# A common tag for the DRAM scratch tensors of cast queries and keys, in a banded-attention and SwiGLU kernel

## The chip, the cores and the metric

The kernel runs on one core of a Trainium2 chip. The metric is the device time of one execution in microseconds (us). Before the change it is 375.43 us, the median of five runs (374.43 to 377.87 us).

## The reference

There are two stages. The first is attention over 8 batches of 8 heads, with 576 positions of 64 numbers each. A query sees the keys within 32 positions of itself and the 8 global positions, and a global query sees every key. The second is a gated feed-forward block over the 4608 rows that result.

```
mask = (abs(pos[:, None] - pos[None, :]) <= 32) | is_global[:, None] | is_global[None, :]
scores = where(mask, q @ k.T / sqrt(64), -1e9)
attn = softmax(scores);  o = attn @ v                    # per batch and head
x = o.transpose(0, 2, 1, 3).reshape(8 * 576, 512)
out = (silu(x @ w_gate) * (x @ w_val)) @ w_out           # 512 -> 1536 -> 512
```

## The kernel before

**Tiling.** All matmuls are in bfloat16. For each batch, `attention(b)` returns a list of steps. Step GT (L362 to L367) transposes the 8 gathered global keys and queries, held in tile `kqm`. Steps S2 and SG (L391, L373) make the scores that involve global positions. Step P2T turns the probabilities of the global queries (tile `p2t`), and step AV2 (L422) multiplies them with the values. Steps S (L452) make the scores of the band, steps AV (L496, L505) multiply with the values `va` and `vb`, and steps X turn the result into `xT`, the input of the feed-forward block. `ffn(t0, n)` takes 512 rows of `xT` at a time: 12 gate units (L638, two groups of four matmuls each) and four output units (L683), so 16 units for each of 9 chunks, 144 in all.

**Order.** The order is written by hand. A counter runs over the 144 units, and after each unit the kernel emits what the dictionary `gaps` holds for that number. Each engine keeps the order in which it was given its instructions. The tiles' pools work out which semaphores an instruction has to wait for.

**Queries and keys.** The score steps need keys and queries turned, with the 64 numbers of a head along the partitions (`kT`, `qT`). For batches 0 to 2 they are loaded into on-chip memory (L80) and turned on TensorE (L344). For batches 3 to 7 they go through DRAM. `cast_qk(b)` (L106 to L110) issues two DMAs on GpSimd's queue that read float32 keys and queries and write them in bfloat16, with positions outermost, to a scratch tensor in DRAM: `kf`, then `qf`. Later `transpose_qk(b)` (L114 to L122) issues two crossbar transposes on SyncE's queue, from `kf` to `kT` (L116) and from `qf` to `qT` (L120). `kT` has two buffers that alternate by batch, and `qT` has two by its pool.

**The scratch tensors.** The pool that they come from is made at L65 with `bufs=1` in DRAM. Before the change each request carries a name of its own (`kf3`, `qf3`, `kf4` and so on) and no tag, so there are ten tensors for five batches.

**When they are issued.** These lines place the steps around the change, by the number of the unit that they follow (`o` is 16 times b - 1):

```
cast_at, tr_at, v_at, g_at, m_at = {3: 12, 4: 25}, {3: 22}, {2: 10}, {2: 8}, {2: 15}
...
            tr_at[b] = o - 16 + 5
...
            cast_at[b] = o - 32 + 8
        v_at[b] = o - 16 + 2
        g_at[b] = o - 16 + 6
        m_at[b] = o - 16 + 13
```

So the transposes of batch b come at units 22, 37, 53, 69 and 85 for b = 3 to 7, and the casts of batches 4 to 7 come three units after the transposes of the batch ahead (25, 40, 56, 72). On GpSimd's queue a cycle is: five loads of `va` for batch b, two gathers of global rows for b (L226), the two casts for b + 1 (L109), and the two small products that make `kqm` for b (L236). GpSimd runs ahead of TensorE, as far as its waits allow. On SyncE's queue a cycle is: two copies that make `vb` (L131, L132), from batch 4 on the crossbar transpose for `p2t` (L408), the transposes of `kf` and `qf` for the next batch, the transposes for `xT` (L540, L562), and the stores of the output (L690).

Of the kernel before, what the change touches and what calls it, by code (L numbers as in the profile page):

```python
# [10 lines left out]
BF16 = mybir.dt.bfloat16  # L11
# [15 lines left out]
def kernel(  # L27
# [13 lines left out]
    B, H, S, D = q.shape  # L41
# [23 lines left out]
    dram = ctx.enter_context(tc.tile_pool(name="dram", bufs=1, space=bass.MemoryType.DRAM))  # L65
# [39 lines left out]

    def cast_qk(b):  # L106
        for name, src in (("k", k), ("q", q)):
            t = dram.tile([S, H, D], BF16, name=f"{name}f{b}")
            nc.gpsimd.dma_start(out=t, in_=src[b].rearrange("h s d -> s h d"))  # L109
            flat[name, b] = t  # L110

# [633 lines left out]
    for f, w in ((transpose_qk, tr_at), (load_v, v_at), (gather_now, g_at), (mask_now, m_at), (cast_qk, cast_at)):  # L745
        for b, n in w.items():
            at(n, f, b)
# [40 lines left out]
```

## Time and profile before

| What | Value |
|---|---|
| median of five runs | 375.43 us (374.43 to 377.87) |
| the profiled execution | 374.88 us |
| its span, first to last instruction | 373.2 us |
| TensorE busy | 346.2 us, 93% of the span |
| VectorE, ScalarE, GpSimd busy | 241.2, 150.7 and 98.2 us |
| granted TensorE clock | 1.000 |
| software DMA queue (GpSimd's) | 19.40 MB, packets take 61.3% of the 16 DMA engines' span |
| hardware DMA queue (SyncE's) | 22.74 MB, 29.7% |

The span runs from the first to the last instruction. The profiled execution took 1.68 us more than its span. A wait in the profile is idle time of an engine, put down to what ended it. A DMA's time to landing runs from its issue to the moment at which its data is complete. SPq and POOLq are the queues of SyncE and GpSimd, PE is TensorE's matmuls, PEld its weight loads, POOL is GpSimd, DVE is VectorE and ACT is ScalarE.

### The profile page before, as it was taken

The numbers are of one execution on the slowest core, as the hardware profiler recorded it, in microseconds if no ns is written. First come the engines' busy times: TensorE is split into PE (matmuls) and PEld (weight loads), VectorE is DVE, ScalarE is ACT, GpSimd is POOL, SyncE is SP. The second block draws the span as 40 slices with busy tenths as digits, with TensorE's granted clock in tenths as the row PEclk, the third lists the DMA queues.
The fourth block names the chain that finished last, engine by engine and source line by source line (L and its number), as shares of the span: only waits on it lengthen the run. The fifth ranks groups of instructions, "written<-read, shape, count | busy, mean of one in ns | idle before, by whom it ended". The sixth has DMA issues, their size and how long they took to land.

```text
span 373.2 us, 7896 instructions
## 1 busy us (share of the span) xinstructions
PE 346.2 (93%) x3224; PEld 175.2 (47%) x3276; DVE 241.2 (65%) x473; ACT 150.7 (40%) x233; POOL 98.2 (26%) x116
## 2 busy tenths in 40 slices
PE   2677999989999999998999999999999999999996
PEld 2464544554454444544554455445544554444442
DVE  5784887268951886488738872887288728724850
ACT  2643474346542652253324442454245423313321
POOL 7966267462127101370128011400000000000000
PEclk9999999999999999999999999999999999999999
DMA  8999999999975994799999998970350032011002
GB/s 117 115 198 201 184 223 140 186 209 138 94 70 85 186 146 61 139 142 149 142 144 138 148 125 141 157 128 18 113 125 2 17 111 52 0 57 58 0 25 88
DMA packets 138835, 42.64 MB, mean 114 GB/s; under 512 B 123824, under 2 KB 133040, under 8 KB 138800
## 3 DMA queue, kind: packets, MB, share of 16 engines
q0 software_dynamic: 93824, 19.40, 61.3%
q1 hardware_dynamic: 44976, 22.74, 29.7%
q8 instruction: 25, 0.41, 0.5%
q14 instruction: 10, 0.08, 0.1%
HBM read 38.28 MB, written 15.34 MB: 144 GB/s over the span
## 4 chain that ended last, share of the span: by engine, by line
PE 79%; DVE 8%; DMA 6%; ACT 3%; issue 2%; POOL 0%; DVEq 0%; POOLq 0%
PE po L683 24%; PE pg L638 21%; PE pv L638 20%; DMA p2t<-p 5%; PE ps_av L496 3%; PE ps_s L452 2%; PE ps_av L505 2%; DVE pt L465 2%; PE ps_t L344 2%; DVE h L676 1%; DMA q_bf<-in_q_dram 1%; DVE gv L672 1%; ACT pe L460 1%; PE ps_x L550 1%; DVE xa L483 1%
## 5 line engine op out<-in xcount | busy, mean ns | idle before, releaser
L638 PE MATMUL pg<-xT,wg_sb 128*128 128x512 bf16 x392 | 106.4, 380 | 3.4 <-issue 1.0
L638 PE MATMUL pv<-xT,wv_sb 128*128 128x512 bf16 x419 | 108.2, 379 | 0.2
L672 DVE SCALAR_TENSOR_TENSOR gv<-th,pg 128x512 bf16<-128x512 bf16 x108 | 74.0, 685 | 36.4 <-ACT th L670 35.5
L670 ACT ACTIVATE th<-pg 128x512 bf16<-128x512 f32 x108 | 64.4, 597 | 82.0 <-PE pg L638 78.0
L683 PE MATMUL po<-wo_sb,h 128*128 128x512 bf16 x417 | 95.5, 379 | 0.7 <-issue 0.3
L676 DVE TENSOR_TENSOR h<-gv,pv 128x512 bf16<-128x512 bf16 x108 | 74.3, 688 | 11.6 <-PE ps_av L505 0.5
L102 POOL DMA_DIRECT2D va<-in_v_dram x40 | 35.2, 913 | 117.5 <-PE ps_av L505 87.0
L638 PEld LDWEIGHTS <-wv_sb 128*128 128x128 bf16 x424 | 41.5, 98 | 50.0
L683 PEld LDWEIGHTS <-h 128*128 128x128 bf16 x432 | 40.8, 98 | 47.5
L638 PEld LDWEIGHTS <-wg_sb 128*128 128x128 bf16 x424 | 37.2, 98 | 41.9 <-issue 2.7
L688 ACT ACTIVATE osb<-po 128x512 f32<-128x512 f32 x36 | 21.5, 597 | 86.1 <-PE po L683 70.6
L460 ACT ACTIVATE pe<-ps_s 128x1024 bf16<-128x1024 f32 (+1 forms) x40 | 37.5, 939 | 17.1 <-PE ps_s L452 16.5
L465 DVE TENSOR_TENSOR pt<-pe,band 128x1024 bf16<-128x1024 bf16 (+1 forms) x40 | 25.5, 637 | 25.5 <-ACT pe L460 25.0
L477 DVE TENSOR_REDUCE den<-ps_av 128x8 f32<-128x16 f32 (+1 forms) x40 | 6.7, 168 | 36.3 <-PE ps_av L505 34.8
L483 DVE TENSOR_TENSOR xa<-ps_av,den 128x512 bf16<-128x512 f32 (+1 forms) x40 | 25.5, 638 | 1.4
L452 PE MATMUL ps_s<-qT,kT 64*128 64x64 bf16 x576 | 16.4, 196 | 3.5 <-ACT pe L460 1.5
L452 PEld LDWEIGHTS <-kT 64*128 64x128 bf16 x576 | 11.6, 98 | 16.9 <-issue 15.3
L496 PE MATMUL ps_av<-gvt,pg 128*64 128x264 bf16 x128 | 18.4, 299 | 1.0 <-DVE gvt L437 1.0
L505 PEld LDWEIGHTS <-pt 128*64 128x64 bf16 x512 | 18.0, 115 | 0.1
L505 PE MATMUL ps_av<-va,pt 128*64 128x66 bf16 x256 | 18.0, 199 | 0.0
L505 PE MATMUL ps_av<-vb,pt 128*64 128x66 bf16 x256 | 18.0, 199 | 0.0
L109 POOL DMA_DIRECT2D qf<-in_q_dram x5 | 14.1, 2826 | 0.0
(98 smaller groups left out, 219.2 us busy)
## 6 DMA issues: line engine op xcount, KB each, us to landing
out_dram<-osb SPq DMA_DIRECT2D x36, 256.0 KB, 2.0
vb<-va SPq DMA_DIRECT2D x14, 264.0 KB, 4.5
va<-in_v_dram POOLq DMA_DIRECT2D x24, 128.0 KB, 5.3
kf<-in_k_dram POOLq DMA_DIRECT2D x5, 576.0 KB, 14.4
qf<-in_q_dram POOLq DMA_DIRECT2D x5, 576.0 KB, 18.3
k_bf<-in_k_dram POOLq DMA_DIRECT2D x6, 288.0 KB, 6.6
q_bf<-in_q_dram POOLq DMA_DIRECT2D x6, 288.0 KB
va<-in_v_dram POOLq DMA_DIRECT2D x16, 96.0 KB, 4.5
```

The lines of the kernel that those rows point to most:

```text
L102: nc.gpsimd.dma_start(out=va[lo:hi, u, :, 0:D], in_=vs[t0 + lo : t0 + hi])
L452: nc.tensor.matmul(out=ps[:, par, 64 * slot : 64 * slot + 64], lhsT=kT[r : r + 64, hp, 64 * t : 64 * t + P], rhs=qTs[b][r : r + 64, hp, 64 ...
L460: nc.scalar.activation(out=pe, in_=ps[:, :, 0 : 64 * ns].rearrange("p r (s c) -> p r s c", c=64), func=AF.Exp, scale=SCALE,)
L465: nc.vector.tensor_tensor(out=pt.rearrange("p r s c -> p (r s) c"), in0=pe.rearrange("p r s c -> p (r s) c"), in1=bc(band, [[0, 2 * ns], [ ...
L483: nc.vector.tensor_tensor(out=xa.rearrange("p (g h) d -> p g h d", g=g), in0=bc(ps, pst + [[1, D]]), in1=bc(den, [[4, g], [1, 4], [0, D]]) ...
L496: nc.tensor.matmul(out=ps[64 * e : 64 * e + 64, hg], lhsT=st["pg"][:, P * tp + 64 * e : P * tp + 64 * e + 64], rhs=st["gv"].rearrange("p h ...
L505: nc.tensor.matmul(out=ps[64 * e : 64 * e + 64, hg, hl, :], lhsT=pt[:, hl % 2, 4 * (hl // 2) + 2 * (tp % 2) + e, :], rhs=(va if e == 0 els ...
L638: nc.tensor.matmul(out=ps[:, 0:n], lhsT=w[:, cc, P * fc : P * (fc + 1)], rhs=xT[:, cc, t0 : t0 + n], start=(cc == 0), stop=(cc == NCC - 1),)
L670: nc.scalar.activation(out=th[:, 0:n], in_=pg[:, 0:n], func=AF.Tanh, scale=0.5)
L672: nc.vector.scalar_tensor_tensor(out=gv[:, 0:n], in0=th[:, 0:n], scalar=1.0, in1=pg[:, 0:n], op0=ALU.add, op1=ALU.mult,)
L676: nc.vector.tensor_tensor(out=st["h"][:, fc, 0:n], in0=gv[:, 0:n], in1=pv[:, 0:n], op=ALU.mult)
L683: nc.tensor.matmul(out=po, lhsT=st["h"][:, fc, P * ts : P * (ts + 1)], rhs=wo_sb[:, fc, :], start=(fc == 0), stop=(fc == NFC - 1),)
```

## The change

The request for a scratch tensor gets a tag that is the same for all batches, `kf` for keys and `qf` for queries, and the batch's number is dropped from the name.

```
 def cast_qk(b):
     for name, src in (("k", k), ("q", q)):
-        t = dram.tile([S, H, D], BF16, name=f"{name}f{b}")
+        t = dram.tile([S, H, D], BF16, tag=f"{name}f", name=f"{name}f")
         nc.gpsimd.dma_start(out=t, in_=src[b].rearrange("h s d -> s h d"))
         flat[name, b] = t
```

Nothing else differs. In the pools of on-chip memory of this kernel, requests with one tag take turns in `bufs` buffers: `qT`, for instance, has one tag and two buffers.

More of the change, by code (lines that the diff above doesn't have):

```diff
@@ L107, in cast_qk @@
         for name, src in (("k", k), ("q", q)):
-            t = dram.tile([S, H, D], BF16, name=f"{name}f{b}")
+            t = dram.tile([S, H, D], BF16, tag=f"{name}f", name=f"{name}f")
             nc.gpsimd.dma_start(out=t, in_=src[b].rearrange("h s d -> s h d"))
```

## The prediction

> **What bounds the kernel now.** I read the shares by engine and the chain that ended last first, to see which engine an added or removed wait has to reach before it counts.
>
> ```profile
> PE 346.2 (93%) x3224; PEld 175.2 (47%) x3276; DVE 241.2 (65%) x473; ACT 150.7 (40%) x233; POOL 98.2 (26%) x116
> ...
> PE 79%; DVE 8%; DMA 6%; ACT 3%; issue 2%; POOL 0%; DVEq 0%; POOLq 0%
> PE po L683 24%; PE pg L638 21%; PE pv L638 20%; DMA p2t<-p 5%; PE ps_av L496 3%; PE ps_s L452 2%; PE ps_av L505 2%; DVE pt L465 2%; PE ps_t L344 2%; DVE h L676 1%; DMA q_bf<-in_q_dram 1%; DVE gv L672 1%; ACT pe L460 1%; PE ps_x L550 1%; DVE xa L483 1%
> ```
>
> TensorE is the bound. GpSimd holds none of the chain, and neither the casts nor the transposes of `kf` and `qf` are in it. A DMA is: `p2t<-p`, 5% of the span. Of TensorE's waits, three tell what the DMAs cost it (us in total, times, longest):
>
> ```profile
> PE ps_av L422 <- DMA p2t<-p: 1.8, 2, 1.1
> ...
> PE ps_t L344 <- DMA q_bf<-in_q_dram: 0.8, 1, 0.8
> ```
>
> No row names `kT<-kf` or `qT<-qf`. The scratch path is early enough to be unseen, and only the wait for `p2t`, 1.8 us, lies where the change could reach: the 0.8 us is at the start, before any cast. Now the two queues in time, first GpSimd's, then SyncE's, around the handover from batch 5 to batch 6 (start, length of the issue, what ended the idle time before):
>
> ```profile
> 160.43 2.33 POOL L109 DMA_DIRECT2D kf<-in_k_dram  x1
> 162.17 2.85 POOL L109 DMA_DIRECT2D qf<-in_q_dram  x1
> 163.90 1.54 POOL L236 TENSOR_TENSOR kqm<-kg,mka 128x128 bf16<-128x128 f32 x1
> 164.26 1.54 POOL L236 TENSOR_TENSOR kqm<-qg,mka 128x128 bf16<-128x128 f32 x1
> 180.16 0.82 POOL L102 DMA_DIRECT2D va<-in_v_dram  x1 [14.36 <-PE ps_av L505]
> ```
> ```profile
> 163.19 2.70 SPq L408 DMA_TRANSPOSE p2t<-p  x1
> 165.99 8.05 SPq L116 DMA_TRANSPOSE kT<-kf  x1
> 174.14 6.36 SPq L120 DMA_TRANSPOSE qT<-qf  x1
> 182.12 1.19 SPq L540 DMA_TRANSPOSE xT<-xa  x1
> ```
>
> The casts of batch 6 go out at 160.43 and 162.17, before the transposes of batch 5 (165.99 and 174.14). So today the cast does not follow the transposes of the batch ahead; it runs beside them. The same holds at 116.92 against 120.99 and at 198.88 against 203.78. An edit that really gave one scratch pair would have to add waits on GpSimd. Whether it does is the whole question.
>
> **The change, part by part.** The edit is a tag and a name. On-chip pools of this kernel hand one tag's buffers round, and a request for a buffer in use brings a wait. So I looked at what becomes of it here: each engine's list of instructions, as the two kernels are built, with the semaphores that every instruction waits for and the values. It is the same list on all five engines. Cast `kf` of batch 4 waits for one semaphore of GpSimd's own queue before and after, that of `qf` for another, and no semaphore of SyncE's queue is added in front of any cast. The storage is the same as well: ten scratch tensors before, ten after, at the same ten addresses, from 81,920 up in steps of 589,824 bytes, which is 576 x 8 x 64 x 2. In this DRAM pool as built a tag doesn't make requests share: each of the ten calls still gets a tensor of its own. What differs is the names.
>
> The absence of a wait would be unsafe if the storage were shared. The Trainium skill, "DMA: Bandwidth & Descriptors", section "Two DMAs through the same engine are not ordered", says that only the completion semaphore orders one DMA behind another. With ten addresses nothing needs ordering, so the two findings fit together. No row of the trace can show it.
>
> The sum: removed 0 instructions, added 0, moved 0. GpSimd's ten casts stay at 2.33 and 2.85 us of issue, SyncE's ten transposes stay where they are, and no wait is added or taken away. Profiled execution 374.88 + 0 = 374.88 us, of which 373.2 is span and 1.68 lies around it. It stands 0.55 below the median of 375.43, and that median is the figure to forecast from: 375.4 us. A cost from both sides: nothing here gives a gain or a loss other than what one program shows between executions, and the five runs show 374.43 to 377.87.
>
> **The rivals.** Each assumes that the tag does share after all, so that `kf` of batch b + 1 is written only when `kT` of batch b has landed, and `qf` when `qT` has.
>
> *Rival 1: the wait is real, is hidden, and relieves the DMA engines.* The one landing that the trace has for `kT` is 14.8 us after issue, for `qT` 11.2. So `qf` of batches 4 to 7, issued today at 82.3, 118.7, 162.2 and 200.6, would go out at 82.2 + 11.2 = 93.4, 129.4 + 11.2 = 140.6, 174.1 + 11.2 = 185.3 and 211.8 + 11.2 = 223.0. Here a rule stands behind the row, and speaks against the change: the same page, section "Anatomy of one DMA — SWDGE (gpsimd) path", has it that DMA engines don't wait on semaphores; the wait is held on the issuing sequencer. So all of GpSimd's queue behind the cast stands too. For batch 6 that is `kqm` of batch 5, from 163.9 to 187.0, and three loads of `va` (180.2, 185.2, 188.9). By the rule GpSimd loses 23.1 us there (187.0 - 163.9); if only the DMA waited, nothing. By the rows it is the same on TensorE: L362 reads this `kqm` at 197.93, 9.4 us after it would be ready (187.0 + 1.5), the `kqm` of batch 4 would come at 142.3 against 159.47 and that of batch 6 at 224.7 against 236.05, and the last `va` load waits for TensorE until 194.6 anyway.
>
> The casts have to land before their transposes: at a median of 18.3 us for `qf`, at 111.7, 158.9, 203.6 and 241.3, against starts at 129.4, 174.1, 211.8 and 243.6. All four fit, by 17.7, 15.2, 8.2 and 2.3 us. So the delay costs 0. What could be gained is seen in the chain between 158 and 176 us, and in how long SyncE's queue holds the last pair, the only one with no cast beside it:
>
> ```profile
> 163.19 9.48 DMA p2t<-p
> 172.67 0.04 issue
> 172.72 0.47 PE ps_av L422 x20
> ```
> ```profile
> 239.89 1.21 SPq L408 DMA_TRANSPOSE p2t<-p  x1
> 241.21 2.34 SPq L116 DMA_TRANSPOSE kT<-kf  x1
> 243.63 3.47 SPq L120 DMA_TRANSPOSE qT<-qf  x1
> ```
>
> `p2t` took 9.48 us beside the casts, and its median landing is 2.6; issues of `kT` take 8.05 us beside them and 2.34 without. Held casts would leave `p2t` at 163.19 and most of that at 201.65 alone. TensorE waits 1.1 + 0.7 = 1.8 us for it, and that is all that can come back: 375.4 - 1.8 = 373.6 us. For it: the text of the change. Against: no wait stands in the built lists. 2 in 100.
>
> *Rival 2, the slower one: the wait is real and closes a loop between the two queues.* The transposes of b + 1 need the casts of b + 1, which need the transposes of b. The loop of the queries takes 11.2 + 18.3 = 29.5 us, while SyncE comes round every 45.2, 45.0, 37.8 and 37.4 us (`kT` at 75.8, 121.0, 166.0, 203.8, 241.2). It decides from a loop over 37.4. Should `qT` stand behind the landing of `kT` (14.8 + 11.2 = 26.0) and the cast take its longest landing, 19.7, the loop is 45.7, and the overruns are 0.5 + 0.7 + 7.9 + 8.3 = 17.4 us. SyncE can be late by 10.6 us (from 243.63 + 3.47 = 247.1 to the next `xT` transpose at 257.72); the other 6.8 hold up `xT`, and TensorE with it: 375.4 + 6.8 = 382.2 us. Against it, besides the lists: `qT` was issued 8.15 us after `kT`, before its 14.8 were over. 1 in 100.
>
> **How the numbers follow.** The same program: 97 in 100, at 375.4. About half a per cent (1.9 us) is what a measurement of this kernel can tell from no change. One run of five lay outside that (377.87), a median of several much more rarely; I give 3 of the 97 to a median that strays, a little more above than below because the outlier is above. Rival 1 (373.6, on the edge of half a per cent) is split between faster and same, rival 2 is slower. Together: faster 0.02, same 0.95, slower 0.03. The range need hold only the first case: half the spread of the five runs is 1.7 us, or 0.46%, for a single run, and I take somewhat less for a median, 374.0 to 376.9. Both rivals lie outside, with 3 in 100.
>
> **What would show it right or wrong.** Right: casts still issued at about 80.6, 116.9, 160.4 and 198.9 us, ahead of the transposes; no row of GpSimd waiting for `kT<-kf` or `qT<-qf`; `kT` issues of about 8 us again, and `p2t` again near 9 us in the chain. Rival 1: casts behind the transposes at 140 and 185 us, GpSimd idle before L109, and TensorE's 1.8 us for `p2t` gone. Rival 2: SyncE idle before L116 or L120 on a cast, and `xT` late. The forecast is wrong if two tensors at different addresses are made to wait for each other by something that is not in the instruction lists.

## The result and the profile after

The changed kernel takes 375.71 us (median of 42 runs, 374.28 to 380.00) against 375.56 us for the kernel before (79 runs). The ratio is 0.9999, with a 95% interval of 0.9984 to 1.0015. The forecast was 375.4 us and no change.

In the profile after, the first lines to read are GpSimd's around the handover from batch 5 to batch 6, and then SyncE's:

```profile
160.69 2.31 POOL L109 DMA_DIRECT2D kf<-in_k_dram  x1
162.43 2.83 POOL L109 DMA_DIRECT2D qf<-in_q_dram  x1
164.16 1.53 POOL L236 TENSOR_TENSOR kqm<-kg,mka 128x128 bf16<-128x128 f32 x1
```
```profile
163.44 2.03 SPq L408 DMA_TRANSPOSE p2t<-p  x1
165.57 7.68 SPq L116 DMA_TRANSPOSE kT<-kf  x1
173.34 6.20 SPq L120 DMA_TRANSPOSE qT<-qf  x1
```

The casts still go out 5 and 3 us before the transpose of `kf` of the batch ahead (165.57), with no idle time in front of them. Here they start within 0.3 us of where they were, and `kT` still takes nearly 8 us to issue. The change does not do what its words say: no cast follows a transpose.

One pair of lines does differ: TensorE's waits for the DMAs, and the chain's share by engine.

```profile
PE ps_av L422 <- DMA p2t<-p: 1.0, 1, 1.0
...
PE ps_t L344 <- DMA q_bf<-in_q_dram: 0.8, 1, 0.8
```
```profile
PE 82%; DVE 8%; DMA 4%; ACT 3%; issue 2%; POOL 0%; DVEq 0%; POOLq 0%
```

TensorE waits 1.0 us for `p2t` instead of 1.8, and the DMAs' share of the chain falls from 6% to 4%. That looks like a small gain with a place and a name, and it is neither. The two programs hold the same instructions, and a later profile of the changed kernel, `e0_changed` below, shows yet other values:

```profile
PE ps_av L422 <- DMA p2t<-p: 0.3, 1, 0.3
```
```profile
PE 83%; DMA 6%; DVE 6%; ACT 3%; issue 2%; POOL 0%; DVEq 0%; POOLq 0%
```

The wait is down to 0.3 us, and the DMAs are back at 6% of the chain. So one program shows both figures at different sizes from one execution to the next, and the share does not follow the wait. Without the instruction lists, a reader could easily have told a story about it.

### The profile page after: what moved, and what is told of

The parts are those of the page before. It is cut to its first block, busy times and chain, and to the rows that moved or that the text cites. A ratio compares the mean times of both kernels' runs of the same rounds, so it can differ in the third digit from the quotient of the medians.

```text
span 372.5 us, 7896 instructions
## 1 busy us (share of the span) xinstructions
PE 346.3 (93%) x3224; PEld 175.4 (47%) x3276; DVE 240.6 (65%) x473; ACT 150.8 (40%) x233; POOL 98.7 (26%) x116
## 4 chain that ended last, share of the span: by engine, by line
PE 82%; DVE 8%; DMA 4%; ACT 3%; issue 2%; POOL 0%; DVEq 0%; POOLq 0%
PE po L683 24%; PE pg L638 22%; PE pv L638 21%; PE ps_s L452 3%; PE ps_av L496 3%; DMA p2t<-p 3%; PE ps_av L505 2%; DVE pt L465 2%; PE ps_t L344 2%; DVE h L676 1%; DMA q_bf<-in_q_dram 1%; DVE gv L672 1%; ACT pe L460 1%; PE ps_x L550 1%; DVE qT L353 1%
## 5 line engine op out<-in xcount | busy, mean ns | idle before, releaser
L102 POOL DMA_DIRECT2D va<-in_v_dram x40 | 35.2, 931 | 115.2 <-PE ps_av L505 83.9
L109 POOL DMA_DIRECT2D qf<-in_q_dram x5 | 14.1, 2823 | 0.0
## 6 DMA issues: line engine op xcount, KB each, us to landing
qf<-in_q_dram POOLq DMA_DIRECT2D x5, 576.0 KB, 19.6
```

The source lines that it names most:

```text
L102: nc.gpsimd.dma_start(out=va[lo:hi, u, :, 0:D], in_=vs[t0 + lo : t0 + hi])
```

## The experiments

Two things were open. Was the time unmoved because nothing is shared, or because a real wait is hidden? And what would a real pair have done? All kernels below keep the line numbers of the listing, except that in those with extra casts L109 issues these and L110 the casts proper. `e3_cast_once` and the kernels with ten tensors and extra casts are made from the changed kernel, the others from the kernel before. In each group the kernel before was run on the same chip, and ratios are to that.

**One real pair.** Two tensors are made once and used by all batches:

```
     flat = {}
+    scratch = {n: dram.tile([S, H, D], BF16, name=f"{n}f") for n in "kq"}
...
-            t = dram.tile([S, H, D], BF16, name=f"{name}f{b}")
+            t = scratch[name]
```

> One scratch pair made once and really used by all five batches; built, it adds eight waits on GpSimd, in front of the casts of batches 4 to 7, each for the transpose of the batch ahead. My theory (the tag shared nothing, which is why the time stood still; a true wait is hidden and frees the DMA engines): kf of batch 6 issued after about 173 to 181 us instead of 160, qf after about 178 to 185, TensorE's wait for p2t down from 1.8 or 1.0 us to near 0, time 373.6 to 375.6 us, ratio 0.995 to 1.000. Rival (the loop between the two queues is over the period): 382 us, SyncE waiting for casts at L116 or L120. Third (the tag did share already): the casts are issued at the same moments as in the changed kernel.

Measured: 371.37 us against 373.60, ratio 0.9942 (0.9917 to 0.9967), just below the ratio expected. The eight waits, GpSimd's idle time at them (us in total, times, longest) and its queue at the same handover, then SyncE's:

```profile
L109 POOLq EVENT_SEMAPHORE  x8: 17/17/17, 88.6 to 210.6; - x8
...
POOL kf L109 <- DMA kT<-kf: 38.6, 4, 11.2
```
```profile
171.66 2.27 POOL L109 DMA_DIRECT2D kf<-in_k_dram  x1 [10.18 <-DMA kT<-kf]
173.63 2.57 POOL L109 DMA_DIRECT2D qf<-in_q_dram  x1
175.36 1.27 POOL L236 TENSOR_TENSOR kqm<-kg,mka 128x128 bf16<-128x128 f32 x1
```
```profile
164.23 1.25 SPq L408 DMA_TRANSPOSE p2t<-p  x1
165.58 2.61 SPq L116 DMA_TRANSPOSE kT<-kf  x1
168.29 2.64 SPq L120 DMA_TRANSPOSE qT<-qf  x1
```

This is what the changed kernel would have looked like; neither the kernel before nor the changed one has a semaphore instruction at L109. Four casts of `kf` wait, 38.6 us in total, each until `kT` of the batch ahead has landed. GpSimd stands for 10.18 us here and TensorE loses nothing by it, because `kqm` is done at about 177 us and L362 reads it at 197.83. `kT` takes 2.61 us to issue instead of 7.68. No row of TensorE waits for the DMA `p2t<-p` any more, and that transpose lands (us from issue, least, median, most) in

```profile
DMA to landing us min/median/max: 2.7/3.6/3.9
```

instead of the 9.48 and 9.14 us that the chain shows in the kernel before. The gain is read best from the distance between equal steps. L362 begins the attention of batches 4 to 7 (start, length), in the kernel before:

```profile
159.47 0.28 PE L362 MATMUL ps_g<-ident,kqm 128*128 128x128 bf16 x2
...
197.93 0.28 PE L362 MATMUL ps_g<-ident,kqm 128*128 128x128 bf16 x2
...
236.05 0.28 PE L362 MATMUL ps_g<-ident,kqm 128*128 128x128 bf16 x2
...
273.35 0.28 PE L362 MATMUL ps_g<-ident,kqm 128*128 128x128 bf16 x2
```

and with one real pair:

```profile
160.52 0.27 PE L362 MATMUL ps_g<-ident,kqm 128*128 128x128 bf16 x2
...
197.83 0.28 PE L362 MATMUL ps_g<-ident,kqm 128*128 128x128 bf16 x2
...
235.13 0.28 PE L362 MATMUL ps_g<-ident,kqm 128*128 128x128 bf16 x2
...
272.43 0.28 PE L362 MATMUL ps_g<-ident,kqm 128*128 128x128 bf16 x2
```

The distances are 38.46, 38.12 and 37.30 us before, and 37.31, 37.30 and 37.30 with the pair. So 37.30 is the undisturbed period, and this profile of before loses 1.16 + 0.82 = 1.98 us, all of it at the two batches whose `p2t` shares the DMA engines with casts. The last period of before has no cast beside it and loses nothing. This profile is at the upper end: read in the same way, four other profiles of kernels whose last casts go out early lose 1.04 (the changed kernel), 0.59 (`e0_changed`), 0.55 (`e2_two_pairs`) and 1.63 us (`e6_first_shared`), 1.2 on average over the five. By the ratios the gain is 1.6 to 2.2 us, here and in two kernels below, one without these casts (`e3_cast_once`) and one that holds the last three (`e7_last_shared`), with intervals that reach down to 0.7. So the periods account for more than half of the gain; that they account for all of it is not shown.

The spans say less here: 372.3 us in this profile of the faster kernel, 369.9 in that of `e0_changed`, because the step GT of batch 2 comes anywhere from 80.3 to 83.9 us after the start, if the kernels with four extra casts are left aside. Why it does so stays open.

**No casts after the first.** `cast_qk` returns at once for the batches after 3 (`XQ` is 3):

```
     def cast_qk(b):
+        if b > XQ: return flat.update({(n, b): flat[n, XQ] for n in "kq"})
```

> Leaves out the casts of batches 4 to 7: their transposes read the scratch of batch 3 again, so the attention of those batches is computed from wrong queries and keys in the bands; everything else runs. It is the ceiling of what freeing the DMA engines of casts can bring. My theory: only TensorE's wait for p2t (1.0 to 1.8 us) is to be had, so 373.6 to 374.6 us, ratio 0.995 to 0.998, with p2t landing in about 2.6 us and issues of kT at 2.3 us. Rival (the chain's 5% share for p2t, 18.6 us, is what the casts cost): 360 us or less.

Measured: 371.69 us against 373.60, ratio 0.9956 (0.9931 to 0.9981). From the DMA line of `p2t` in this kernel (us from issue to landing, least, median, most):

```profile
DMA to landing us min/median/max: 2.6/3.4/4.1
```

Leaving the casts out brings no more than holding them back. The ceiling is about 2 us, and one real pair reaches it within the intervals. The 5% that the chain gave to `p2t` in the kernel before was 18.6 us of elapsed transfer (9.48 + 9.14) with TensorE at work beside nearly all of it. The idle time in front of L422 was the figure to use.

**The changed kernel again, and two real pairs.** `e0_changed` is the changed kernel itself. `e2_two_pairs` takes two real pairs in turn:

```
+    scratch = {(n, i): dram.tile([S, H, D], BF16, name=f"{n}f{i}") for n in "kq" for i in (0, 1)}
...
+            t = scratch[name, b % 2]
```

> The changed kernel once more, beside the others on the same chip. My theory (it is the program of before under other names): ratio to the kernel before within 0.002 of 1, casts of batches 4 to 7 issued before the transposes of the batch ahead. Rival (the names or the tag do something that the lists don't show): ratio of 0.996 or less, or 1.004 or more.

> Two real scratch pairs taken in turn: six waits stand in front of the casts of batches 5, 6 and 7, but each is for the transposes of two batches ahead, which have landed long before. My theory (what gains in the kernel with one pair is the moment of the cast, not the number of tensors or their addresses): ratio 0.997 to 1.002, casts issued at the same moments as before, TensorE waiting 1 to 2 us for p2t. Rival (fewer scratch tensors, or addresses used again, are faster by themselves): 0.994 as with one pair.

Measured: `e0_changed` 373.80 against 373.85 us, ratio 0.9999 (0.9973 to 1.0025). `e2_two_pairs` 374.79 us, 1.0025 (0.9991 to 1.0059). In both, the casts go out at about 79.6, 115.0, 158.5 and 196.1 us, ahead of the transposes. In this profile of two pairs TensorE waits only 0.4 us for `p2t`, not the 1 to 2 expected; that is within what the kernel before and the changed one show (0.3 to 1.8). Two pairs are shared storage with six waits in front of the casts, and bring nothing, since each wait is over before it is reached. So neither storage used again nor a wait as such is what gains in the kernel with one pair; the later moment of the cast is.

**Which handover gains.** Either only batches 3 and 4 share a pair (`scratch[name, max(b - 4, 0)]` of four), or only batches 4 to 7 do (`scratch[name, int(b > 3)]` of two). The reason to ask: the stage between the steps GT of batches 2 and 3 took 40.40 us in the profile of before, and 39.57 and 39.50 in the two faster kernels.

> Only batches 3 and 4 share a pair, batches 5 to 7 have their own, so only the first handover is held. It separates the two places where the kernel with one pair gained: here the stage between the steps GT of batches 2 and 3 should take 39.5 us instead of 40.4, and the waits for p2t (1 to 2 us) should stay. Time about 0.8 us below before, ratio 0.997 to 0.999. If the 0.8 us came by chance with the chip, no gain, and the stage stays at 40.4.

> The other part: batch 3 has its own pair and batches 4 to 7 share one, so the last three handovers are held. The waits for p2t should be gone and the steps GT of batches 4 to 7 stand 37.3 us apart; the stage between the steps GT of batches 2 and 3 should keep its 40.4 us. Ratio 0.995 to 0.997. If the gain of the kernel with one pair lies in the first handover alone: ratio 0.998 or more.

Measured: the first handover alone 373.87 us, ratio 0.9999 (0.9968 to 1.0030); the last three alone 372.07 us, 0.9957 (0.9933 to 0.9981). The gain is in the last three, where the periods are 37.30, 37.30 and 37.31 us; for the first alone the interval leaves room for 0.3% at most. My 0.8 us in the first handover did not hold: the stage takes 39.50 us in both kernels, but also in `e0_changed`, where no cast is held. The 0.9 us appears in the profiles of before and after from the first measurements only, as a late start of ScalarE's `kT` copy of batch 2 (idle 1.51 us in both). Where it comes from stays open; held casts are not the reason.

**Longer casts.** The slower rival said that a real pair closes a loop between the two queues. To lengthen the loop, two or four more casts of the keys into unused tensors stand between `kf` and `qf` in every batch, once with one real pair, once with ten tensors:

```
+            for i in range(2 * (name == "q")): nc.gpsimd.dma_start(out=dram.tile([S, H, D], BF16, name=f"pad{b}_{i}"), in_=k[b].rearrange("h s d -> s h d"))
```

> One real pair as in the kernel with one pair, and two more casts of the keys to unused scratch between kf and qf, in all five batches, to lengthen the loop between the queues. By the loop model: two casts add about 20 us to the 29.5, so about 45 to 50 us against a period of 37.4 in the last two handovers: SyncE waits at L120 for qf in batches 6 and 7, xT comes late, 380 to 392 us. Rival (a late scratch pair is hidden by how early the transposes are placed, 12 units ahead of their use): within 1% of the kernel with the same extra casts and ten tensors.

> Control: ten tensors as before, with the same two extra casts between kf and qf in all five batches. By the loop model nothing closes: qf of batch 6 lands at about 162 + 40 = 202 us against its transpose at 211.8, so the cost is only what the extra traffic does to p2t and to the loads of values: 375 to 379 us. Rival (the extra traffic itself is what costs in the kernel with one pair and the extra casts): the same time as that kernel.

Measured with two extra casts: one pair 371.58 us, ratio 0.9965 (0.9941 to 0.9990); ten tensors 373.60 us, 0.9995 (0.9971 to 1.0019). Both expectations failed: the pair should have taken 380 us or more, and ten tensors 375 or more. There is no overrun, and the gain of the real pair is still there although twice as much is cast. The durations point to the reason. In the kernel with one pair the landings of `kT` are

```profile
DMA to landing us min/median/max: 4.7/6.0/10.9
```

and in its four handovers a held `kf` lands in 8.0 to 8.5 us, a held `qf` in 10.0 to 10.9. The loop of the rival had used 14.8, 11.2 and 18.3, all of them from a profile in which casts and transposes ran together.

> One real pair and four extra casts of the keys to unused scratch between kf and qf, in all five batches. In the kernel with two extra casts a held cast landed in 8 to 10 us, so the loop of the queries was about 8 us (start to landing of kT) plus 4 casts at 8.3 = 41 us, of which the first batches' slack took the rest. With four extra casts it is 8 + 6 x 8.3 = 58 us against a period of 37.3. My theory (the slower rival's mechanism is real, only its durations were too long, so it closes only when the casts are about twice as much): qf of batch 6 lands at about 169 + 50 = 219 us, after the xT transpose due at 216, and qf of batch 7 at about 270, 16 us after the xT transpose due at 254; time 385 to 400 us. Rival (the scratch pair has no path to the end at all): within 1% of before.

> Control with ten tensors and the same four extra casts. The casts of a batch take 6 x 8.3 = 50 us of the software queue against a period of 37.3, so this queue alone falls behind, but without the 8 us in which it waits for kT: qf of batch 6 at about 158 + 50 = 208 us (its transpose is due at 211), qf of batch 7 at about 259, 3 us after the next xT transpose. Time 376 to 388 us, at least 8 us below the kernel with one pair and the same extra casts, if the wait is what costs there; the same time if only the traffic does.

Measured with four extra casts: one pair 397.94 us against 373.48, ratio 1.063 (1.058 to 1.069). That is in the expected range, but by luck, as the waits show. With ten tensors four runs took 390.04, 397.33, 397.74 and 397.76 us, all above the 388 at which the expected range ends. I had expected the pair to be at least 8 us slower. Three of these runs lie within 0.7 us of it and the quickest lies 7.9 us below, so four runs do not decide whether sharing costs anything here. The profile with ten tensors is that of the run of 397.74 us. These are the waits of the kernel with one pair, GpSimd's, TensorE's:

```profile
POOL kf L110 <- DMA kT<-kf: 40.4, 3, 15.2
POOL pad L109 <- issue: 27.8, 10, 5.4
POOL qf L110 <- issue: 20.4, 5, 8.7
```
```profile
PE ps_g L362 <- POOL kqm L236: 18.0, 2, 9.1
```

and of the one with ten tensors:

```profile
POOL pad L109 <- issue: 49.2, 11, 9.8
POOL kf L110 <- DMA qf<-in_q_dram: 19.7, 4, 9.3
POOL qf L110 <- issue: 19.6, 5, 8.3
```
```profile
PE ps_g L362 <- POOL kqm L236: 18.0, 2, 9.4
```

By these rows GpSimd stands 40.4 + 27.8 + 20.4 = 88.6 us at its casts in the one and 49.2 + 19.7 + 19.6 = 88.5 in the other. With this many casts GpSimd comes to a stand in these two profiles whether or not a tensor is shared, and the wait for `kT` takes the place of other waits. What ends the stands marked `issue` the profile does not show; I take them for waits for room in the queue, which no run here tests. The harm falls on `kqm`, two small products queued behind the casts: TensorE waits 18.0 us for them, in both. In the kernel before, `kqm` of batch 5 was done at about 166 us and read at 197.93. The first of the two waits is at batch 2, behind the casts of batch 3, where not even one real pair has anything to wait for.

The granted clock was 0.970 and 0.974 in these two profiles, and it is low in and just after TensorE's longest waits. With one pair TensorE waits for `kqm` until 89.90 and 257.03 us. In the 5 us after these moments (90 to 95, 257 to 262) the clock is 0.61 and 0.58, and in the next 5 us it is 1.00 again. After the wait of 2.7 us for `xT`, which ends at 168.25, it is 0.66 (168.3 to 173.3), then 1.00. So each of TensorE's long waits cost more than its length: by these clocks about 2 us of full-speed work each, an estimate (5 x 0.39, 5 x 0.42 and 5 x 0.34 us).

## Why the prediction was right, step by step

- **The sum of nothing.** Right. No wait was added, the casts of batches 4 to 7 went out at 80.9, 117.2, 160.7 and 198.0 us (80.6, 116.9, 160.4 and 198.9 before), and 375.71 us was measured for 375.4. `p2t` took 9.36 us in the chain, as forecast. (The prediction speaks of three waits of TensorE for DMAs; the trace has the two that it shows.) The step that carried it was the instruction list with its semaphores and addresses; the profile of before could not have decided it, and from the words of the change alone rival 1 would have been the answer.
- **The tag does not share in this DRAM pool.** Right: two tensors made by hand add the eight waits and the tag adds none, with the same pool and `bufs=1`. Why this pool gives each request a tensor of its own, no run here shows.
- **Rival 1, had the change done what it says.** The mechanism was right. Its term of 1.8 us measured 2.2 us (373.60 x 0.0058, interval 1.2 to 3.1). That the two come so close is in part luck, since the 1.8 us is one profile's figure and others of the same program show 1.0 and 0.3. The gain came at the batches where I had put it. By its times the rival was too pessimistic: I expected `qf` at 185.3 us, and it went out at 173.6. The failing step was to take landings of 14.8 and 11.2 us from a trace in which casts and transposes ran together, for a kernel in which they would not. The slack of 2.3 us at the last handover was really some 21 us: `qf` went out at 211.2, landed in 10.6, and was read at 242.7.
- **The rule against the change.** That the wait holds up GpSimd and what is queued behind it is seen in every handover of the real pair (6.8 us of GpSimd at the first, 10 to 11 at the last three, where 23.1 had been worked out for one). It costs TensorE nothing, as the rows had said.
- **Rival 2.** Its loop had the same wrong durations, and two extra casts did not close it. Its place was wrong too. When the casts finally cost 24 us, 18.0 us of TensorE's waits stood at `kqm`, and only 2.7 us at `xT`. Whether sharing had a part in it is not decided: the kernel with ten tensors lost as much in three runs of four.

## What to carry to other kernels

Before pricing a wait, look in the built instruction lists whether it is there: a tag that makes two requests share in one pool may not do so in another. A transfer's duration from a trace with contention must not be used to price the schedule that would remove the contention. A DMA's share of the chain is elapsed transfer, not what it costs: 5% of the chain stood beside waits of 1.8 us in one profile and 0.3 in another. If this kernel is to have what the change promised, a scratch pair made once by hand brings it: 371.37 us, 0.6% under the kernel before, whose time the changed kernel has. Casts that wait for the transposes stay out of the way of the short transpose on TensorE's path.

## What was not expected of the hardware

- The crossbar transpose of `p2t` lands in 2.6 to 4.1 us with no cast beside it (the one landing on record in the kernel before, and all four in the kernel without casts after the first) and takes 8.5 to 9.5 us beside one (the kernel before and both profiles of the changed kernel). In the kernel before a cast of 576 KB lands in 14.4 to 19.7 us; held until `kT` has landed it takes 8.0 to 10.9. Held one behind the other, casts and transposes are done no later than together at the one handover where both are on record, the last: the last of them lands at 211.80 + 11.2 = 223.0 us in the kernel before and at 211.19 + 10.6 = 221.8 with the pair, though its casts start 10 us later.
- The same program lost between 0.3 and 1.8 us of TensorE's time to this in three profiles (1.8, 1.0 and 0.3). The share of the chain does not follow: `p2t` has 5.0%, 2.5% and 4.7% there.
- GpSimd stops when enough casts are queued: up to 9.8 us in front of a single issue with four extra casts. What ends such a stop the profile does not show.
- After a wait of TensorE of 2.7 to 9 us the granted clock was 0.58 to 0.66 for the next 5 us, and 1.00 again after that (four extra casts, one pair).
